# The tail of an attention and two-layer block: where z is widened and the tokens are split

## The chip, the cores and the metric

One core of one Trainium2 chip runs the whole kernel. The metric is the device time of one execution in microseconds (us), the median of several runs. The engines are TensorE (PE in the rows, its weight loads PEld), VectorE (DVE), ScalarE (ACT), GpSimd (POOL) and SyncE (SP), which issues most DMAs.

## The reference

The input passes through three stages; the change touches the last one only.

```
scores = q @ k^T / sqrt(D), masked to a window (half of the heads: a dilated one)
x   = softmax(scores) @ v                 # 2304 tokens x 512
h   = x @ w_in;  y = (h - tanh(h)) @ w_out          # 512 -> 2048 -> 512
h2  = y @ w_in2                                     # 512 -> 1024
sm  = softmax(h2);  s = h2 * sm
ln  = (s - mean(s)) / sqrt(var(s) + 1e-6) * g_ln
out = ln @ w_out2                                   # 1024 -> 512
```

## The kernel before

The order of instructions on each engine is the order of the program text; nothing reorders it. An engine that waits holds up all that stands behind it in its queue. Waits between engines are put in by the framework from what is read and written; a buffer of a pool is handed on when its last reader is done.

Attention and the middle layer are untouched; they end at about 507 us. The last stage works on nine pairs of token tiles of 128 (NP = 9, pairs 0 to 8). A pair has two tiles: 2i+1, called o in the text, and 2i, called e.

The **first product** of pair i, `mm3(i)` at L639, is h2 by a scheme of seven products instead of eight, with sums of blocks of y and of w_in2. Each product (`prod`, L615) is six matmuls of 512 columns, since each operand is split in a high and a low part and three of the four combinations are used. Four PSUM banks are used in turn: b0, b1, b2, b3. ScalarE copies b0 to c (L652); VectorE forms u2 (L653) and u3 (L658); four `neg_add` (L636) write the negated halves of both tiles to hn and keep a running minimum. The bank b1 is used again (product p4) once u2 has read it, b3 (p2) once u3 has read it. The list `mid` holds two hooks: hook 0 runs after b2's product and before u3, hook 1 after the first tile's minima. Behind them are the exponential (`softmax_e`, L681), the product with it (`softmax_u`, L686), the mean's removal (`softmax_z`, L692 and L693) and the sum of squares (`square`, L702).

The **second product**, `mm4` at L754, is 24 matmuls for each tile from z, the transposed and split normalised tile; its result is scaled by the factor g on ScalarE (L764) and written out by SP (L765).

z comes in one of two ways. `trz` (L723) transposes hn by TensorE into PSUM and splits it from there (L733, L734); pair 0 uses this. `split_z` (L736) makes a high and a low half of 16 bits (ScalarE L740, VectorE L741), SP starts a transposing DMA (L744), and `put_z` (L746) widens both halves (ScalarE L751, VectorE L752). In that way the tile is scaled by the factor f (column 4 of `sml`), in the first it is not, and `rest` multiplies g by it.

The **tokens' split**, `split_y(j, parts)` at L519, prepares y of pair j. Part 0 makes four differences on GpSimd (L530), one of them into y's own buffer, then casts one half (VectorE L537) and subtracts (GpSimd L538). Part 2 casts the other half, in which the fourth difference lies, and part 1 the sums; each has its L537 and L538. `load_y(j)` (L514) loads y of pair j by SP into the only buffer `yr`, which must have been read by the split of pair j-1. `fac` (L704) and `rest` (L710) make the factors f and g by small GpSimd instructions of [128x1].

The loop at L779 goes over the pairs: the factors and `split_z` of pair i+1, the second product of pair i, the first product of pair i+2. There the split of pair i+3 starts in hook 0 and is ended in the next turn of the loop, ahead of `split_z`.

Of the kernel before, what the change touches and what calls it, by code (L numbers as in the profile page):

```python
# [40 lines left out]
def tile_kernel(ctx: ExitStack, tc: tile.TileContext, qk, vw, cst, w_in, w_out, w_in2, w_out2, g_ln, out):  # L41
# [470 lines left out]
    NP = NTOK // YT  # L512

    def load_y(j):  # L514
        if j < NP:
            y_raw[j] = p2.tile([128, KD, YT], F32, tag="yr", name=f"yr{j}", bufs=1)
            nc.sync.dma_start(out=y_raw[j], in_=y_dr[:, :, j * YT:(j + 1) * YT])

    def split_y(j, parts=range(3)):  # L519

        if j >= NP:
            return
        r = y_raw[j]
        if 0 in parts:
            y = yt[j] = p2.tile([128, 2, 7, 2, TT], F32R, tag="yt", name=f"yt{j}")
            sm = y_sm[j] = p2.tile([128, 3, 2, TT], F32, tag="ysm", name=f"ysm{j}", bufs=1)
            a11, a21, a22 = r[:, 0:2, 0:TT], r[:, 0:2, TT:YT], r[:, 2:4, TT:YT]
            for o, a, b, op in ((sm[:, 0], a21, a22, ALU.add), (sm[:, 1], sm[:, 0], a11, ALU.subtract),
                                (sm[:, 2], a11, a21, ALU.subtract), (a21, r[:, 2:4, 0:TT], sm[:, 1], ALU.subtract)):
                nc.gpsimd.tensor_tensor(out=o, in0=a, in1=b, op=op)  # L530
        y, sm = yt[j], y_sm[j]
        yh = y[:, 0].rearrange("p s k t -> p (s k) t")
        yl = y[:, 1].rearrange("p s k t -> p (s k) t")
        for p, sl, v in ((0, slice(0, 4), r[:, :, 0:TT]), (2, slice(4, 8), r[:, :, TT:YT]),
                         (1, slice(8, 14), sm.rearrange("p s k t -> p (s k) t"))):
            if p in parts:
                nc.vector.tensor_copy(out=yh[:, sl], in_=v)  # L537
                nc.gpsimd.tensor_tensor(out=yl[:, sl], in0=v, in1=yh[:, sl].bitcast(F32), op=ALU.subtract)  # L538
        if 2 in parts:
            y_raw.pop(j)  # L540
            y_sm.pop(j)
# [73 lines left out]
    def prod(ps, y, blk, w, first=True):  # L615

        q = 0
        for kk in range(2):
            for a, b in ((0, 0), (0, 1), (1, 0)):
                nc.tensor.matmul(ps, y[:, a, blk, kk], w2i[w, kk][:, b], start=first and q == 0, stop=q == 5,  # L620
                                 skip_group_check=not first)
                q += 1

    def bank(pool, tag, i, nm):
        return pool.tile([128, 512], F32, tag=tag, name=f"s{nm}_{i}")

    def neg_add(i, t, n, a, b):

        d = st[2 * i + t]
        if "hn" not in d:  # L630
            d["hn"] = p3.tile([128, FF2], F32, tag="hn", name=f"hn{2 * i + t}", bufs=3)
            d["sml"] = p3.tile([128, 8], F32, tag="sml", name=f"sml{2 * i + t}", bufs=6)
            init, acc = 3.0e38, d["sml"][:, 7:8]
        else:
            init, acc = d["sml"][:, 7:8], d["sml"][:, 0:1]
        nc.vector.tensor_tensor_reduce(out=d["hn"][:, n * 512:(n + 1) * 512], in0=a, in1=b, op0=ALU.add, op1=ALU.min,  # L636
                                       scale=-1.0, scalar=init, accum_out=acc)

    def mm3(i, mid=()):  # L639

        y = yt.pop(i)
        for t in range(2):
            st[2 * i + t] = {}
        mid = dict(mid)
        b0, b1 = bank(sa, "b0", i, "p1"), bank(sa, "b1", i, "p6")
        prod(b0, y, 0, "b11")
        prod(b1, y, 5, "t2")
        u2 = p3.tile([128, 512], F32, tag="u2", name=f"u2_{i}", bufs=1)
        u3 = p3.tile([128, 512], F32, tag="u3", name=f"u3_{i}", bufs=1)
        b2, b3 = bank(sb, "b2", i, "p5"), bank(sb, "b3", i, "p7")  # L650
        c = p3.tile([128, 512], F32, tag="c", name=f"c_{i}", bufs=1)
        nc.scalar.copy(out=c, in_=b0)  # L652
        nc.vector.tensor_tensor(out=u2, in0=b1, in1=c, op=ALU.add)  # L653
        prod(b2, y, 4, "t1")
        if 0 in mid:
            mid[0]()
        prod(b3, y, 6, "t3")
        nc.vector.tensor_tensor(out=u3, in0=b3, in1=u2, op=ALU.add)  # L658
        neg_add(i, 1, 1, b2, u3)
        b1 = bank(sa, "b1", i, "p4")  # L660
        prod(b1, y, 3, "t4")
        neg_add(i, 1, 0, b1, u3)
        if 1 in mid:
            mid[1]()
        softmax_e(2 * i + 1)
        b3 = bank(sb, "b3", i, "p2")
        prod(b3, y, 1, "b21")
        neg_add(i, 0, 0, b3, c)
        softmax_u(2 * i + 1)
        prod(b2, y, 2, "b22", first=False)  # L670
        neg_add(i, 0, 1, b2, u2)
        softmax_e(2 * i)
        softmax_z(2 * i + 1)
        square(2 * i + 1)
        softmax_u(2 * i)
        softmax_z(2 * i)
# [33 lines left out]
    def rest(i):  # L710

        d = st[i]
        ssum, sc, var, g = (d["sml"][:, c:c + 1] for c in (1, 4, 5, 6))
        nc.gpsimd.tensor_scalar(out=ssum, in0=ssum, scalar1=1e-9, scalar2=1e-3, op0=ALU.add, op1=ALU.mult)
        nc.gpsimd.tensor_tensor(out=ssum, in0=ssum, in1=ssum, op=ALU.mult)
        nc.gpsimd.tensor_tensor(out=ssum, in0=ssum, in1=var, op=ALU.add)
        nc.gpsimd.tensor_tensor(out=ssum, in0=ssum, in1=half, op=ALU.pow)
        nc.gpsimd.tensor_tensor(out=var, in0=var, in1=sc, op=ALU.mult)
        nc.gpsimd.tensor_tensor(out=g, in0=ssum, in1=var, op=ALU.mult)
        if i < 2:  # L720
            nc.gpsimd.tensor_tensor(out=g, in0=g, in1=sc, op=ALU.mult)

    def trz(i):  # L723

        d = st[i]
        z = d["z"] = p3.tile([128, 2, NF2, TT], F32R, tag="z", name=f"z{i}")
        for n in range(2):
            ps = zo.tile([128, 512], F32, tag="zp", name=f"zp{i}_{n}").rearrange("p (j t) -> p j t", t=TT)
            for j in range(4):
                c = 4 * n + j  # L730
                nc.tensor.transpose(ps[:, j], d["hn"][:, c * TT:(c + 1) * TT], ident)
            zh, zl = z[:, 0, 4 * n:4 * n + 4], z[:, 1, 4 * n:4 * n + 4]
            nc.scalar.copy(out=zh, in_=ps)  # L733
            nc.vector.tensor_tensor(out=zl, in0=ps, in1=zh.bitcast(F32), op=ALU.subtract)  # L734

    def split_z(i):  # L736

        d = st[i]
        ab = p3.tile([128, 2, FF2], F16, tag="ab", name=f"ab{i}")
        nc.scalar.activation(out=ab[:, 0], in_=d["hn"], func=AF.Copy, scale=d["f"])  # L740
        nc.vector.scalar_tensor_tensor(out=ab[:, 1], in0=d["hn"], scalar=d["f"], in1=ab[:, 0], op0=ALU.mult,  # L741
                                       op1=ALU.subtract)
        t = d["zt"] = p3.tile([128, 2 * NF2, TT], F16, tag="zt", name=f"zt{i}")
        nc.sync.dma_start_transpose(out=t, in_=ab.rearrange("p a n -> p (a n)"))  # L744

    def put_z(i):  # L746

        d = st[i]
        z = d["z"] = p3.tile([128, 2, NF2, TT], F32R, tag="z", name=f"z{i}")
        t = d["zt"].rearrange("p (a j) t -> p a j t", a=2)  # L750
        nc.scalar.copy(out=z[:, 0], in_=t[:, 0])  # L751
        nc.vector.tensor_copy(out=z[:, 1], in_=t[:, 1])  # L752

    def mm4(i):  # L754
        d = st.pop(i)
        z = d["z"]
        po = zo.tile([128, DM], F32, tag="po", name=f"po{i}")
        q = 0
        for j in range(NF2):
            for a, b in ((0, 0), (0, 1), (1, 0)):  # L760
                nc.tensor.matmul(po, z[:, a, j], w2o[j][:, b], start=(q == 0), stop=(q == 3 * NF2 - 1))  # L761
                q += 1
        o = p3.tile([128, DM], F32, tag="o", name=f"o{i}")
        nc.scalar.activation(out=o, in_=po, func=AF.Copy, scale=d["g"])  # L764
        nc.sync.dma_start(out=out[i * TT:(i + 1) * TT, :], in_=o)  # L765

    mm3(0)
    fac(1)

# [9 lines left out]
    for i in range(NP):  # L779
        o, e = 2 * i + 3, 2 * i + 2  # L780
        if i + 1 < NP:
            square(e)
            fac(o)
            fac(e)
        split_y(i + 2, (1, 2))
        load_y(i + 3)
        if i + 1 < NP:
            split_z(o)
            split_z(e)
            rest(o)  # L790
            rest(e)
        mm4(2 * i + 1)
        if i + 1 < NP:
            put_z(o)
        mm4(2 * i)
        if i + 2 < NP:
            mm3(i + 2, {0: lambda: split_y(i + 3, (0,)), 1: lambda: put_z(e)})
        elif i + 1 < NP:
            put_z(e)
    p2.release()  # L800
    sa.release()

# [74 lines left out]
```

## Time and profile before

| | us |
|---|---|
| median of 3 runs | 721.9 (721.08 to 724.3) |
| the profiled execution | 726.59 |
| its span | 724.8 |
| TensorE busy | 690.9 (95%) |
| VectorE busy | 484.2 (67%) |
| ScalarE busy | 384.3 (53%) |
| GpSimd busy | 204.8 (28%) |

Times in the rows are us from the start of the span. A row in order of time begins with its start and its duration; where the engine stood idle just before, the idle time and what ended it stand at its end in brackets. The granted clock of TensorE is a share of its full speed of 2.4 GHz; the other level is 1.2 GHz.

### The profile page before, as it was taken

The page shows a single profiled execution, that of the slowest core. Times are in us where ns is not written, and L with a number is a line of the kernel's source. Part 1 is how long each engine was busy: PE and PEld are TensorE (multiplying, and loading weights), DVE is VectorE, ACT ScalarE, POOL GpSimd, SP SyncE. Part 2 cuts the span into 40 slices and gives each one's busy share as a digit, 9 for nine tenths or more (in the row PEclk, how much of TensorE's full clock was granted, in tenths as well). Part 3 has the DMA queues.
Part 4 walks back from the last instruction along what each step waited for, and adds up shares of the span by engine and source line. Part 5 has one row for each costly group of instructions (what it writes and reads, how often), then busy time and mean ns, then how long its engine had stood idle before and what let it go on. Part 6 is the DMA issues. An engine that isn't in the chain of part 4 may idle for free.

```text
span 724.8 us, 11261 instructions
## 1 busy us (share of the span) xinstructions
PE 690.9 (95%) x3978; PEld 636.4 (88%) x3978; DVE 484.2 (67%) x1157; ACT 384.3 (53%) x917; POOL 204.8 (28%) x274
## 2 busy tenths in 40 slices
PE   6898999999999999999999999999998989989987
PEld 5688999999999999999999999999876768777766
DVE  5987667476667766666667424998676757766760
ACT  5778776465555555555546433655444344534551
POOL 2312321111011111110011102661194774557530
PEclk9999999999999999999999999999999999999997
DMA  9985521232222122322112004532113551254322
GB/s 267 338 267 180 189 85 55 65 110 66 67 66 90 53 66 66 110 66 66 45 65 67 1 10 165 189 130 104 44 35 82 116 117 45 73 116 117 76 60 67
DMA packets 63591, 72.41 MB, mean 100 GB/s; under 512 B 36272, under 2 KB 50096, under 8 KB 63536
## 3 DMA queue, kind: packets, MB, share of 16 engines
q1 hardware_dynamic: 60368, 66.98, 31.9%
q10 hardware_dynamic: 3168, 4.72, 1.8%
q8 instruction: 31, 0.51, 0.3%
q14 instruction: 24, 0.20, 0.1%
HBM read 53.86 MB, written 9.44 MB: 87 GB/s over the span
## 4 chain that ended last, share of the span: by engine, by line
PE 73%; DVE 8%; DMA 6%; ACT 5%; issue 4%; POOL 2%; SPq 0%; ACTq 0%; POOLq 0%; DVEq 0%
PE y L381 28%; PE h L354 28%; PE sp L620 5%; DMA zt<-ab 5%; PE po L761 3%; PE pv L281 2%; PE qkp L205 2%; PE tp L260 2%; PE qkp L225 2%; ACT e L681 1%; DVE hn L636 1%; DMA qkr<-in_qk_dram 1%; DVE hn L686 1%; ACT e L702 1%; ACT ab L740 1%
## 5 line engine op out<-in xcount | busy, mean ns | idle before, releaser
L354 PE MATMUL h<-x,wi 128*128 128x384 f32 x1152 | 222.2, 341 | 1.3 <-DVE t L365 1.3
L381 PE MATMUL y<-gs,wo 128*128 128x384 f32 x1152 | 219.1, 339 | 0.0
L381 PEld LDWEIGHTS y<-gs,wo 128*128 128x128 f32 x1152 | 201.5, 189 | 1.8
L354 PEld LDWEIGHTS h<-x,wi 128*128 128x128 f32 x1152 | 200.2, 189 | 2.7 <-DVE t L365 1.5
L253 POOL TENSOR_TENSOR p<-p,rs 96x512 f32<-96x512 f32 x47 | 57.3, 1219 | 353.9 <-DVE rs L251 332.0
L761 PE MATMUL po<-w2o_o,z 128*128 128x512 f32 x432 | 103.2, 399 | 3.2 <-ACT z L751 3.2
L365 DVE TENSOR_TENSOR t<-h,t 128x384 f32<-128x384 f32 x96 | 53.0, 552 | 78.6 <-ACT t L362 78.5
L761 PEld LDWEIGHTS po<-w2o_o,z 128*128 128x128 f32 x432 | 83.1, 193 | 22.0 <-ACT z L751 3.6
L371 DVE TENSOR_TENSOR gs<-t,gs 128x384 fp32r<-128x384 f32 x96 | 82.6, 861 | 23.3 <-ACT gs L368 23.2
L362 ACT ACTIVATE t<-h 128x384 f32<-128x384 f32 x96 | 47.0, 489 | 93.9 <-PE h L354 90.6
L245 ACT ACTIVATE p<-p,nm 96x128 f32<-96x128 f32 x192 | 75.0, 393 | 21.5 <-DVE nm L210 21.1
L368 ACT CAST gs<-t 128x384 fp32r<-128x384 f32 x96 | 49.0, 510 | 49.4 <-DVE t L365 49.1
L620 PE MATMUL sp<-w2i_t,yt 128*128 128x512 f32 x216 | 56.0, 410 | 13.2 <-DVE u L653 12.5
L620 PEld LDWEIGHTS sp<-w2i_t,yt 128*128 128x128 f32 x216 | 41.4, 195 | 25.0 <-DVE u L653 15.4
L741 DVE SCALAR_TENSOR_TENSOR ab<-hn,sml,ab 128x1024 f16<-128x1024 f32 x16 | 37.4, 2375 | 14.2 <-ACT ab L740 14.2
L681 ACT ACTIVATE e<-hn,sml 128x1024 f32<-128x1024 f32 x18 | 20.8, 1154 | 44.9 <-DVE sml L636 26.2
L751 ACT CAST z<-zt 128x1024 fp32r<-128x1024 f16 x16 | 16.8, 1048 | 49.8 <-DMA zt<-ab 49.6
L620 PE MATMUL sp<-w2i_b,yt 128*128 128x512 f32 x162 | 41.5, 403 | 0.0
L620 PEld LDWEIGHTS sp<-w2i_b,yt 128*128 128x128 f32 x162 | 32.1, 199 | 7.2
L205 PE MATMUL qkp<-qkr 64*96 64x128 f32 x160 | 29.4, 339 | 7.8 <-DMA qkr<-in_qk_dram 6.6
L245 ACT ACTIVATION_READ_ACCUMULATOR p<-p,nm 96x1 f32 x192 | 36.2, 189 | 0.0
L205 PEld LDWEIGHTS qkp<-qkr 64*96 64x96 f32 x160 | 24.1, 205 | 12.4 <-DMA qkr<-in_qk_dram 6.0
(89 smaller groups left out, 844.9 us busy)
## 6 DMA issues: line engine op xcount, KB each, us to landing
qkr<-in_qk_dram SPq DMA_DIRECT2D x28, 448.0 KB, 3.3
raw_wi<-in_w_in_dram SPq DMA_DIRECT2D x16, 511.8 KB, 7.5
raw_wo<-in_w_out_dram SPq DMA_DIRECT2D x16, 511.8 KB, 7.5
v<-in_vw_dram SPq DMA_DIRECT2D x48, 128.0 KB, 3.3
y_dr<-ys ACTq DMA_DIRECT2D x6, 768.0 KB, 3.9
yr<-y_dr SPq DMA_DIRECT2D x9, 512.0 KB, 4.7
out_dram<-o SPq DMA_DIRECT2D x18, 256.0 KB, 2.2
qkr<-in_qk_dram SPq DMA_DIRECT2D x20, 224.0 KB, 5.4
```

The source lines that it names most:

```text
L205: nc.tensor.matmul(ps[:, b], d["r"][:64, b * NQ:(b + 1) * NQ], d["r"][:64, QC + b * NK:QC + (b + 1) * NK], start=True, stop=True)
L245: nc.scalar.activation(out=d["p"][:, b], in_=d["p"][:, b], func=AF.Exp, scale=-1.0, bias=d["nm"][:, b:b + 1], accum_out=d["sm"][:, b:b + 1])
L253: eng.tensor_tensor(out=d["p"], in0=d["p"], in1=d["rs"].unsqueeze(2).to_broadcast([NQ, 4, NK]), op=ALU.mult)
L354: nc.tensor.matmul(ps, w[:, a, k * 128:(k + 1) * 128], xt[g, k][:, b], start=(n == 0), stop=(n == 3 * KD - 1))
L362: nc.scalar.activation(out=t, in_=ps, func=AF.Tanh)
L365: nc.vector.tensor_tensor(out=t, in0=ps, in1=t, op=ALU.subtract)
L368: nc.scalar.copy(out=gs[:, 0], in_=t)
L371: nc.vector.tensor_tensor(out=gs[:, 1], in0=t, in1=gs[:, 0].bitcast(F32), op=ALU.subtract)
L381: nc.tensor.matmul(yb[g][m], wo[c][:, a, m * 128:(m + 1) * 128], gs[:, b], start=(c == 0 and i == 0), stop=(c == NF - 1 and i == 2))
L620: nc.tensor.matmul(ps, y[:, a, blk, kk], w2i[w, kk][:, b], start=first and q == 0, stop=q == 5, skip_group_check=not first)
L741: nc.vector.scalar_tensor_tensor(out=ab[:, 1], in0=d["hn"], scalar=d["f"], in1=ab[:, 0], op0=ALU.mult, op1=ALU.subtract)
L761: nc.tensor.matmul(po, z[:, a, j], w2o[j][:, b], start=(q == 0), stop=(q == 3 * NF2 - 1))
```

## The change

Three things are changed. From the fourth pair on (first product i = 3, which splits pair 4) all of the split of the next pair stands inside the first product, part 0 ahead of c and u2 and parts 2 and 1 behind u2, with the load of the pair after that behind it; the splits of pairs 2 and 3 stay where they were, but the loads of pairs 3 and 4 now stand behind `split_z` and `rest`. The widening of o's z moves from between the two second products into hook 0 of the next first product. For the last pair, z of both tiles is transposed by TensorE (`trz`) behind the second products of pair 7, and `rest` multiplies its g by the factor.

```diff
@@ mm3 @@
         prod(b0, y, 0, "b11")
         prod(b1, y, 5, "t2")
+        if i > 2:
+            split_y(i + 1, (0,))
...
         nc.scalar.copy(out=c, in_=b0)
         nc.vector.tensor_tensor(out=u2, in0=b1, in1=c, op=ALU.add)
+        if i > 2:
+            split_y(i + 1, (1, 2))
+            load_y(i + 2)
         prod(b2, y, 4, "t1")
@@ rest @@
-        if i < 2:
+        if i // 2 in (0, NP - 1):
             nc.gpsimd.tensor_tensor(out=g, in0=g, in1=sc, op=ALU.mult)
@@ loop over the pairs @@
-        split_y(i + 2, (1, 2))
-        load_y(i + 3)
-        if i + 1 < NP:
+        if i < 2:
+            split_y(i + 2, (1, 2))
+        if i + 2 < NP:
             split_z(o)
             split_z(e)
+        if i + 1 < NP:
             rest(o)
             rest(e)
+        if i < 2:
+            load_y(i + 3)
         mm4(2 * i + 1)
-        if i + 1 < NP:
-            put_z(o)
+        if i + 2 == NP:
+            trz(o)
         mm4(2 * i)
+        if i + 2 == NP:
+            trz(e)
         if i + 2 < NP:
-            mm3(i + 2, {0: lambda: split_y(i + 3, (0,)), 1: lambda: put_z(e)})
-        elif i + 1 < NP:
-            put_z(e)
+            mm3(i + 2, {0: lambda: (put_z(o), i == 0 and split_y(3, (0,))), 1: lambda: put_z(e)})
```

## Rows read from the trace of the kernel before

**Rows 1.** Costliest groups of the page: busy, mean ns, idle before and its releaser.
```profile
L620 PE MATMUL sp<-w2i_t,yt 128*128 128x512 f32 x216 | 56.0, 410 | 13.2 <-DVE u L653 12.5
...
L751 ACT CAST z<-zt 128x1024 fp32r<-128x1024 f16 x16 | 16.8, 1048 | 49.8 <-DMA zt<-ab 49.6
```
**Rows 2.** In order of time, VectorE, pairs 2, 3, 7 and 8.
```profile
549.53 0.68 DVE L658 TENSOR_TENSOR u<-sp,u 128x512 f32<-128x512 f32 x1
...
555.38 0.75 DVE L636 CUSTOM_DVE_ANT_0 hn<-sp,u,sml 128x512 f32<-128x512 f32 x1
...
572.12 0.69 DVE L653 TENSOR_TENSOR u<-sp,c 128x512 f32<-128x512 f32 x1 [1.38 <-ACT c L652]
...
573.44 0.68 DVE L658 TENSOR_TENSOR u<-sp,u 128x512 f32<-128x512 f32 x1
...
578.28 0.75 DVE L636 CUSTOM_DVE_ANT_0 hn<-sp,u,sml 128x512 f32<-128x512 f32 x1
...
672.29 0.75 DVE L636 CUSTOM_DVE_ANT_0 hn<-sp,u,sml 128x512 f32<-128x512 f32 x1
...
693.34 0.75 DVE L636 CUSTOM_DVE_ANT_0 hn<-sp,u,sml 128x512 f32<-128x512 f32 x1
```
**Rows 3.** In order of time, TensorE's weight loads and last matmuls.
```profile
597.32 2.21 PEld L620 LDWEIGHTS sp<-w2i_t,yt 128*128 128x128 f32 x6 [4.03 <-DVE u L653]
...
602.63 10.94 PEld L761 LDWEIGHTS po<-w2o_o,z 128*128 128x128 f32 x48
...
644.74 4.24 PEld L620 LDWEIGHTS sp<-w2i_b,yt 128*128 128x128 f32 x12
...
706.88 14.02 PE L761 MATMUL po<-w2o_o,z 128*128 128x512 f32 x48 [3.16 <-ACT z L751]
```
**Rows 4.** Stretches: PE, PEld, DVE, ACT, POOL busy, clock, DMA share, GB/s.
```profile
576.90:602.63 25.73, 22.12 (x91) 17.81 (x90) 16.36 (x28) 10.63 (x17) 14.27 (x23) 0.93 0.40 82
...
692.35:724.80 32.45, 25.39 (x98) 19.99 (x96) 8.57 (x14) 10.19 (x14) 6.65 (x16) 0.87 0.26 65
```
**Rows 5.** The transpositions of pair 0: ns min/median/max, first and last start.
```profile
L731 PE MATMUL zp<-cst_sb,hn x16: 271/273/273, 521.5 to 525.9; 128*128 128x128 f32 x16
```
**Rows 6.** In order of time, the second run of eight transpositions.
```profile
525.15 1.04 PE L731 MATMUL zp<-cst_sb,hn 128*128 128x128 f32 x8
```
**Rows 7.** In order of time, SP: the transposing DMAs' issue in the first two pairs.
```profile
540.79 5.14 SPq L744 DMA_TRANSPOSE zt<-ab  x2
...
564.27 5.63 SPq L744 DMA_TRANSPOSE zt<-ab  x2
```
**Rows 8.** The loads of L517, from issue to landing.
```profile
DMA to landing us min/median/max: 4.3/4.6/4.9
```
**Rows 9.** In order of time, GpSimd: a split's first and last steps, the last factor.
```profile
571.01 0.73 POOL L530 TENSOR_TENSOR ysm<-yr 128x256 f32<-128x256 f32 x1
...
574.08 1.29 POOL L538 TENSOR_TENSOR yt<-yr,yt 128x512 fp32r<-128x512 f32 x1
...
705.28 0.19 POOL L719 TENSOR_TENSOR sml<-sml 128x1 f32<-128x1 f32 x1
```
**Rows 10.** In order of time, VectorE and GpSimd where they overlap.
```profile
622.46 1.29 POOL L538 TENSOR_TENSOR yt<-yr,yt 128x512 fp32r<-128x512 f32 x1
...
623.23 1.07 DVE L752 CAST z<-zt 128x1024 fp32r<-128x1024 f16 x1
...
680.04 2.84 POOL L538 TENSOR_TENSOR yt<-ysm,yt 128x768 fp32r<-128x768 f32 x1
...
681.09 2.87 DVE L741 SCALAR_TENSOR_TENSOR ab<-hn,sml,ab 128x1024 f16<-128x1024 f32 x1
```
**Rows 11.** VectorE's casts from 500 us on: ns min/median/max, first and last start.
```profile
L537 DVE CAST yt<-yr x14: 417/422/803, 524.3 to 676.5; 128x512 fp32r<-128x512 f32 x14
L537 DVE CAST yt<-ysm x7: 552/553/555, 535.3 to 676.9; 128x768 fp32r<-128x768 f32 x7
...
L752 DVE CAST z<-zt x16: 687/694/1073, 546.2 to 708.1; 128x1024 fp32r<-128x1024 f16 x16
```

## The prediction

> **What bounds the kernel now.** I read the busy shares by stage first, then the costliest groups, then the tail in order of time; the change touches nothing before about 540 us. The page shows who waits: ScalarE's widening of z idles 49.8 us for the transposing DMA, and the matmuls of the first product idle 13.2 us, 12.5 of it for u2 [rows 1]. In order of time the reason is plain: the copy c of the next first product stands behind the widening of z in ScalarE's queue, so u2 comes only after the DMA (572.12 for u2, 573.44 for u3 [rows 2]), while TensorE waits up to 4.03 us and then loads six weights in 2.21 us [rows 3]. That stretch of 25.73 us has a mean granted clock of 0.93, so part of it ran at 1.2 instead of 2.4 GHz [rows 4]. With no wait, a pair is 90 matmuls at 10.94/48 us = 20.5 us [rows 3].
>
> I count in one mark, N: the start of the last minimum of a pair (neg_add on the other tile's second half). Before, N is 555.38 for pair 2, 578.28 for pair 3, 672.29 for pair 7 and 693.34 for pair 8 [rows 2]. So pairs 4 to 7 took 94.0 us, 23.5 each, 3.0 over TensorE's 20.5. That is the most that the change can win there, 12 us in all, and only if nothing else takes the place of the DMA wait.
>
> **The end: a gain.** The last two second products wait 3.16 us for z and then take 14.02 us for 48 matmuls, which at full clock are 10.94 [rows 3]. From the start of pair 7's second product (692.35 [rows 4]) to the last matmul (720.90) is 28.6 us. After, TensorE makes both transpositions itself: 96 matmuls, 21.9 us, and 16 transpositions. The nearest row has 16 of them as single instructions of 0.27 us that issue in two runs of eight, a run 1.04 us; I take 2.1 us, at most 16 x 0.27 = 4.4 [rows 5, 6]. 24.1 us in all: 4.5 us are won (2.2 at the upper bound). The four evictions of each transposition on ScalarE and VectorE lie beside a second product of 5.5 us; the added multiplication by sc is one [128x1] on GpSimd, long before it is needed. Both at nothing.
>
> **Pairs 2 and 3: a loss in the changeover.** load_y(3) and load_y(4) move from ahead of the two transposing DMAs in SP's queue to behind them. SP is held by these two for 5.14 us from 540.79 and 5.63 us from 564.27 [rows 7]. So load_y(3) is issued at 545.9, some 6 us later than before, and lands 4.6 us later [rows 8], at 550.6. The split's cast stands ahead of u3 in VectorE's queue, so u3, which was at 549.53 [rows 2], starts at about 551.2, and pair 2's N goes from 555.4 to about 556.4.
>
> Pair 3 is worse, since its whole split now stands inside its own first product (the changed code takes "i > 2" in the fourth one): the cast of part 0 is ahead of u2, the two others ahead of u3. SP is done with the transposing DMAs at 569.9 [rows 7]; plus the 1.0 us of pair 2, less some 0.5 as no load competes with them, load_y(4) is issued at 570.5 and lands at 575.2. u2, which was at 572.12, comes at 576. What is late next is u3. GpSimd's four differences start when the load has landed and take 3.1 us (571.01 to 574.08 [rows 9]), 0.3 more for the cast beside them: 578.6. Only then may VectorE cast parts 2 and 1.
>
> **What the casts cost there.** VectorE and GpSimd don't run side by side on SBUF here. A widening that takes 0.69 us alone took 1.07 where GpSimd's L538 was on: it began at 623.23 and ended at 624.30, 0.55 after L538 ended at 623.75 [rows 10]. The split of z that began at 681.09 ended at 683.96, 1.08 after the L538 that ended at 682.88 [rows 10]. The cast is 0.42 alone and up to 0.80 [rows 11]. I read this as a whole instruction of one holding the other up. The Trainium skill says so too (SBUF — State Buffer, "SBUF: two separate sides"): the shared pair of ports is an exclusive lock, taken for the instruction by whichever engine starts first. By that rule the sum below holds; if the two only shared, rival A's sum would.
>
> With it, from the end of the differences: GpSimd's L538 of part 0 follows at once (1.3), the cast of part 2 waits it out and needs 0.3 more, the cast of part 1 about 0.5, then L538 of part 2, waiting since the first cast, goes ahead (1.2), and only then VectorE's widening of z (0.55 left of 0.69 [rows 11]): 3.8 us until u3, against 0.42 + 0.55 + 0.69 = 1.6 with no hold-up. u3 of pair 3 is at 582.4. From u3 to N the old pair 3 took 4.84 us (573.44 to 578.28 [rows 2]); I take 5.1, since TensorE has idled 4 us ahead of its last 12 matmuls, and such 12, 2.7 us at full clock, took 4.24 behind one wait [rows 3]. N of pair 3 is 587.5, 9.2 us later than before.
>
> **Pairs 4 to 7: a new chain of the same length.** The DMA is off the path: by pair 8's rows z is usable 13.5 us after N (693.34 to 706.88 [rows 2, 3]), early enough. But GpSimd's queue now holds, in this order, both fac, both rest, the four differences, three L538. The factors end 12.1 us after N (pair 8's last one at 705.28 + 0.19, and there too no L538 stood between [rows 9]); the differences need 3.1; then 3.8 as above to u3; then 4.84 to 5.1 to the next N: 12.1 + 3.1 + 3.8 + 5.0 = 24.0 us, against 23.5. Four pairs: +2.0 us. Bounds: 21.8 without the hold-up, 24.8 if the last 12 matmuls run at the lower clock and the small GpSimd steps lose a us more. I take 24.0, as both rows of an overlap show the whole hold-up. load_y(j+2) behind that split on SP is free: the next transposing DMAs come some 8 us later, and it lands long before the next split.
>
> Pair 8 has no split beside it, so there TensorE decides: 20.5 us from pair 7's second product, which starts about 0.7 us ahead of N. From N of pair 7 to pair 8's end this is 19.8 against 20.1 (672.29 to 692.35 [rows 2, 4]): -0.3.
>
> **The sum.** +9.2 (changeover) + 2.0 (pairs 4 to 7) - 0.3 (pair 8) - 4.5 (end) = +6.4 us. The profiled execution took 726.59 with its span of 724.8, 4.7 over the median of the runs; I add the difference to the median: 721.9 + 6.4 = 728.3.
>
> **Rivals.**
> A. The casts are not held up. u3 of pair 3 comes at 580.0 and N at 585.0 (+6.7), pairs 4 to 7 take 21.8 each (-6.8): 6.7 - 6.8 - 0.3 - 4.5 = -4.9, 717.0 us, faster. For it: u2 and the minima, which read PSUM, run beside GpSimd undelayed. Against: the overlaps above [rows 10, 11]. Chance 0.17.
> B. Held up once, not twice: the widening of z gets in ahead of L538 of part 2. 22.9 a pair, pair 3 at +8.0: 8.0 - 2.4 - 0.3 - 4.5 = +0.8, 722.7, no change. It decides by who goes when a cast ends. Against: L538 of part 1 at 680.04 took 2.84, far more than 1.5 times the 1.29 of one of two thirds its size [rows 10], so there VectorE got in between two of GpSimd's, the one that waits first. Chance 0.18.
> C. load_y(4) lands in time for the fourth split. Then the differences start when the factors end, at about 572.1 instead of 575.2, and 3.1 us fall away: +3.3, 725.2. Against: SP's order. Chance 0.08.
> D. 24.8 a pair: +9.6, 731.5. For it: TensorE now idles 3.6 us in every pair, and its clock fell in both stretches with waits as long. Chance 0.12.
> The forecast has 0.45.
>
> **How the numbers follow.** A measurement tells 0.5% (3.6 us: 718.3 to 725.5) from no change. Slower: the forecast's and D's, less what their own spread brings below 725.5, with part of C: 0.58. Same: B, most of C and the edge of the forecast: 0.24. Faster: A and a little of B: 0.18. The forecast's own range is 725 to 731; 717 to 732 leaves out about half of A and some of D.
>
> **What would show it.** Right: u2 of the fourth pair at about 576, its u3 past 582; the wait for z from the DMA gone from ScalarE, and in its place VectorE's casts waiting for GpSimd's differences and lasting up to 1.3 us longer than alone; TensorE idle before p2 (b3), not before p4; about 24 us from N to N; TensorE without a gap in the last 24 us and at full clock. Wrong: N to N at 21.8 or less, or load_y(4) issued ahead of the transposing DMAs.

## The result: slower by 1.5%, and why the range just missed it

Before 721.49 us (median of 4), after 732.68 (median of 4, 730.74 to 734.97): the ratio is 1.015, 95% interval 1.0107 to 1.0194. Timed once more side by side on another occasion, the two took 721.94 and 733.86, ratio 1.0147 (1.0117 to 1.0177). Slower was forecast, by 6.4 us; it is 11 to 12, and the median lies 0.7 above the range.

The profiled executions stand nearer to the forecast: the span went from 724.8 to 731.8, 7.0 more, at the same mean granted clock of 0.985. So the chain that was worked out is there nearly step by step, and most of the miss is in what before's profiled execution was taken for. Both are shown below.

**The profile after.** In order of time on VectorE, the fourth first product (u2, now L655, to u3, now L663), then N of pairs 2 to 7, which answer to [rows 2]:

```profile
575.76 0.43 DVE L537 CAST yt<-yr 128x512 fp32r<-128x512 f32 x1 [7.30 <-DMA yr<-y_dr]
576.10 0.68 DVE L655 TENSOR_TENSOR u<-sp,c 128x512 f32<-128x512 f32 x1
579.11 1.48 DVE L537 CAST yt<-yr 128x512 fp32r<-128x512 f32 x1 [2.32 <-POOL yr L530]
580.50 0.55 DVE L537 CAST yt<-ysm 128x768 fp32r<-128x768 f32 x1
580.97 1.75 DVE L757 CAST z<-zt 128x1024 fp32r<-128x1024 f16 x1
582.64 0.68 DVE L663 TENSOR_TENSOR u<-sp,u 128x512 f32<-128x512 f32 x1
...
556.81 0.74 DVE L636 CUSTOM_DVE_ANT_0 hn<-sp,u,sml 128x512 f32<-128x512 f32 x1
...
588.10 0.75 DVE L636 CUSTOM_DVE_ANT_0 hn<-sp,u,sml 128x512 f32<-128x512 f32 x1
...
611.77 0.75 DVE L636 CUSTOM_DVE_ANT_0 hn<-sp,u,sml 128x512 f32<-128x512 f32 x1
...
636.04 0.75 DVE L636 CUSTOM_DVE_ANT_0 hn<-sp,u,sml 128x512 f32<-128x512 f32 x1
...
659.70 0.75 DVE L636 CUSTOM_DVE_ANT_0 hn<-sp,u,sml 128x512 f32<-128x512 f32 x1
...
683.96 0.75 DVE L636 CUSTOM_DVE_ANT_0 hn<-sp,u,sml 128x512 f32<-128x512 f32 x1
```

VectorE waits 7.30 us for y of pair 4 (the row shows the wait ahead of the cast) and 2.32 us for GpSimd's differences; u2 is at 576.10 (forecast: 576), u3 at 582.64 (582.4), N of pair 3 at 588.10 (587.5). From there N to N is 23.67, 24.27, 23.66 and 24.26 us (24.0).

SP shows where the load stands, to be read beside [rows 7]:

```profile
565.70 4.75 SPq L749 DMA_TRANSPOSE zt<-ab  x2
570.56 0.99 SPq L517 DMA_DIRECT2D yr<-y_dr  x1
```

The load is issued when the second transposing DMA has left SP, at 570.56 (forecast: 570.5).

All engines in order of time, pair 5's split inside the fifth first product:

```profile
602.58 0.74 POOL L530 TENSOR_TENSOR yr<-yr,ysm 128x256 f32<-128x256 f32 x1
...
603.28 1.30 POOL L538 TENSOR_TENSOR yt<-yr,yt 128x512 fp32r<-128x512 f32 x1
603.36 1.50 DVE L537 CAST yt<-yr 128x512 fp32r<-128x512 f32 x1 [0.86 <-POOL yr L530]
604.78 0.55 DVE L537 CAST yt<-ysm 128x768 fp32r<-128x768 f32 x1
604.94 1.52 POOL L538 TENSOR_TENSOR yt<-yr,yt 128x512 fp32r<-128x512 f32 x1 [0.36 <-DVE yt L537]
605.25 1.76 DVE L757 CAST z<-zt 128x1024 fp32r<-128x1024 f16 x1
606.42 2.27 POOL L538 TENSOR_TENSOR yt<-ysm,yt 128x768 fp32r<-128x768 f32 x1
...
606.93 0.68 DVE L663 TENSOR_TENSOR u<-sp,u 128x512 f32<-128x512 f32 x1
```

This is the double hold-up of the forecast. The cast of part 2 starts 0.08 us behind GpSimd's L538 and ends 0.28 us after it; it takes 1.50, and alone 0.42 [rows 11]. L538 of part 2, whose row starts at 604.94, goes ahead of the widening of z, which takes 1.76 instead of 0.69. From the end of the differences (603.32) to u3 it is 3.61 us; 3.8 was the forecast.

TensorE's weight loads and last matmuls, beside [rows 3]:

```profile
576.84 2.21 PEld L620 LDWEIGHTS sp<-w2i_t,yt 128*128 128x128 f32 x6 [4.45 <-DVE u L655]
...
583.37 4.17 PEld L620 LDWEIGHTS sp<-w2i_b,yt 128*128 128x128 f32 x12 [4.33 <-DVE u L663]
...
607.67 2.59 PEld L620 LDWEIGHTS sp<-w2i_b,yt 128*128 128x128 f32 x12 [2.31 <-DVE u L663]
...
631.31 4.10 PEld L620 LDWEIGHTS sp<-w2i_b,yt 128*128 128x128 f32 x12 [3.27 <-DVE u L663]
...
709.57 1.03 PE L736 MATMUL zp<-cst_sb,hn 128*128 128x128 f32 x8
...
716.74 11.25 PE L766 MATMUL po<-w2o_o,z 128*128 128x512 f32 x48
```

The wait for u2 ahead of p4 has become a wait for u3 ahead of p2 in the pairs that carry a split; pair 3 has both (4.45 and 4.33 us). ScalarE still idles for z's DMA, 14.4 us in all instead of 49.6, but no u2 waits for its copy c any more. At the end TensorE transposes in runs of 1.03 us and has its last 48 matmuls at full clock, 11.25 instead of 14.02.

### The profile page after: what moved, and what is told of

The parts are those of the page before. It is cut to its first block, busy times and chain, and to the rows that moved or that the text cites. A ratio compares the mean times of both kernels' runs of the same rounds, so it can differ in the third digit from the quotient of the medians.

```text
span 731.8 us, 11282 instructions
## 1 busy us (share of the span) xinstructions
PE 692.7 (95%) x3994; PEld 638.2 (87%) x3994; DVE 479.0 (65%) x1157; ACT 383.9 (52%) x917; POOL 205.8 (28%) x276
## 4 chain that ended last, share of the span: by engine, by line
PE 73%; DVE 9%; POOL 8%; issue 4%; ACT 3%; DMA 2%; SPq 0%; ACTq 0%; POOLq 0%; DVEq 0%
PE y L381 28%; PE h L354 26%; PE po L766 6%; PE sp L620 5%; PE pv L281 2%; PE tp L260 2%; PE qkp L225 2%; PE qkp L205 2%; POOL ysm L530 1%; DMA yr<-y_dr 1%; POOL yt L538 1%; DVE z L757 1%; DVE hn L636 1%; DVE p L210 1%; ACT e L686 1%
## 5 line engine op out<-in xcount | busy, mean ns | idle before, releaser
L766 PE MATMUL po<-w2o_o,z 128*128 128x512 f32 x432 | 100.7, 392 | 0.0
L766 PEld LDWEIGHTS po<-w2o_o,z 128*128 128x128 f32 x432 | 81.1, 188 | 17.7
L245 ACT ACTIVATE p<-p,nm 96x128 f32<-96x128 f32 x192 | 75.2, 394 | 21.2 <-DVE nm L210 20.8
L620 PE MATMUL sp<-w2i_b,yt 128*128 128x512 f32 x162 | 46.6, 440 | 17.3 <-DVE u L663 17.3
L620 PEld LDWEIGHTS sp<-w2i_b,yt 128*128 128x128 f32 x162 | 34.3, 216 | 27.7 <-DVE u L663 20.1
L620 PE MATMUL sp<-w2i_t,yt 128*128 128x512 f32 x216 | 52.6, 398 | 4.8 <-DVE u L655 4.0
L292 DVE TENSOR_TENSOR x<-pv,x 128x384 fp32r<-128x384 f32 x24 | 16.4, 703 | 25.7 <-ACT x L290 25.2
L746 DVE SCALAR_TENSOR_TENSOR ab<-hn,sml,ab 128x1024 f16<-128x1024 f32 x14 | 22.2, 1630 | 15.9 <-ACT ab L745 15.9
```

The source lines that it names most:

```text
L245: nc.scalar.activation(out=d["p"][:, b], in_=d["p"][:, b], func=AF.Exp, scale=-1.0, bias=d["nm"][:, b:b + 1], accum_out=d["sm"][:, b:b + 1])
```

## Experiments

One table for all profiled executions, worked out from N (its start, on VectorE) and from the end of the last matmul, in us. The first number is the time of N of pair 1; the next three columns are from N to N; the last one is the median of before's own runs that were timed beside that kernel. Rows with the same one were timed together.

| kernel | N of pair 1 | pair 2 | pair 3 | pairs 4-7 | N of pair 7 to last matmul | median | before's |
|---|---|---|---|---|---|---|---|
| before | 530.74 | 24.64 | 22.90 | 94.01 | 48.61 | 721.49 | |
| before again | 530.78 | 24.49 | 22.32 | 92.98 | 47.57 | 724.28 | 723.94 |
| before, third | 531.50 | 26.07 | 22.76 | 91.42 | 47.35 | (one) 724.79 | 721.94 |
| after | 530.51 | 26.30 | 31.29 | 95.86 | 44.03 | 732.68 | 721.49 |
| after again | 532.88 | 26.33 | 32.27 | 94.52 | 43.21 | 733.86 | 721.94 |
| loads back | 529.00 | 22.48 | 27.47 | 95.67 | 44.25 | 724.40 | 723.94 |
| low order | 528.95 | 26.39 | 30.25 | 91.98 | 44.26 | 728.38 | 721.94 |
| end only | 530.73 | 24.87 | 22.50 | 93.20 | 44.22 | 720.15 | 721.94 |
| widening only | 529.53 | 22.40 | 20.11 | 84.86 | 45.88 | 709.06 | 723.94 |
| widening and end | 528.78 | 22.48 | 20.98 | 86.07 | 42.95 | 706.29 | 723.94 |

**Before, again.** No edit.

> The kernel before, unchanged, profiled once more. Open: the profiled execution of before took 726.59 us, 5 over the median of its runs, while that of the changed kernel took 733.56, about its median. Theory 1: TensorE's clock fell in more pairs of the last stage in that execution than in a usual one (stretches of 25.98, 25.73 and 24.43 us with a mean granted clock of 0.93 beside 21.9 to 22.4 at 1.00); then a faster execution shows fewer such stretches, its mean clock over the span is above 0.985, and the runs' times go down as their clocks go up. Theory 2: the excess lies ahead of 530 us; then the stretches of the last stage are as before and the last stage starts some us earlier.

Ratio 1.000 (0.998 to 1.002). Its profiled execution, with a clock of 0.991, took 723.83 us. Pair 6's first product, that of [rows 3] at 644.74, shows the difference (weight loads, then the last matmuls):

```profile
642.58 1.23 PEld L620 LDWEIGHTS sp<-w2i_t,yt 128*128 128x128 f32 x6 [2.40 <-DVE u L653]
643.88 2.67 PEld L620 LDWEIGHTS sp<-w2i_b,yt 128*128 128x128 f32 x12
...
705.13 13.01 PE L761 MATMUL po<-w2o_o,z 128*128 128x512 f32 x48 [3.13 <-ACT z L751]
```

The twelve loads that took 4.24 us in the first profile take 2.67 here, and the last 48 matmuls 13.01 instead of 14.02. Up to N of pair 1 the two agree within 0.04 us. Of the executions of before that were timed beside it, the three with a clock of 0.985 took 726.17 to 726.92, the three with 0.995 took 720.95 to 722.50. So the 726.59 of the first profile (0.985) is one of the slowest that this kernel has on record, by the clock in its last stage: theory 1.

**The widening only.** Before, with the widening of o's z in hook 0 and nothing else:

```diff
         mm4(2 * i + 1)
-        if i + 1 < NP:
+        if i + 2 == NP:
             put_z(o)
         mm4(2 * i)
         if i + 2 < NP:
-            mm3(i + 2, {0: lambda: split_y(i + 3, (0,)), 1: lambda: put_z(e)})
+            mm3(i + 2, {0: lambda: (put_z(o), split_y(i + 3, (0,))), 1: lambda: put_z(e)})
```

> Before, with one part of the change alone: the widening of o's z moves into hook 0 of the next first product, ahead of the split's part 0; the split, the loads and the end stay as they were. Theory (the split's move and not that of the widening is what lost the time): c and u2 no longer wait for the transposing DMA, the factors and the split stay where VectorE and GpSimd had time for them, a pair takes 20.6 to 22 us from N to N instead of 23.5, TensorE hardly waits: faster by 9 to 16 us, 706 to 713. Rival (the widening in hook 0 is itself late, since u3 stands behind it): a pair stays at 23 to 24 us and the time within 3 us of before.

709.06 us, ratio 0.9826 (0.9775 to 0.9877): the theory holds. Pairs 4 to 7 take 84.9 us, 21.2 each. So this part of the change, alone, is worth some 13 to 15 us; what loses it again is the move of the split and of its loads, which the next runs take apart.

**The widening and the end.** The edit above, with the change's own edit of the end (`trz` for pair 8).

> Before, with the move of the widening and with TensorE's transposition of the last pair, without the split's and the loads' move. Theory: the gains add, 4.5 us on top of the one before: 701 to 709. Rival (the widening in hook 0 is late): 4.5 us faster than before at most, 717.

706.29 us, ratio 0.9775 (0.9744 to 0.9807), the fastest of all, 17.7 us under before and some 26 under the changed kernel. The end adds 2.8 us to the gain of the widening alone, where 4.5 were expected. Stretches from one second product to the next (the columns of [rows 4]):

```profile
548.84:569.81 20.97, 20.96 (x92) 16.75 (x90) 16.61 (x26) 10.64 (x16) 14.34 (x24) 1.00 0.42 101
569.81:594.22 24.41, 22.23 (x92) 17.59 (x91) 18.35 (x28) 11.07 (x17) 15.93 (x25) 0.95 0.41 87
594.22:615.11 20.89, 20.89 (x92) 17.18 (x91) 15.10 (x23) 10.76 (x15) 14.24 (x23) 0.98 0.43 102
615.11:635.88 20.77, 20.77 (x91) 16.82 (x90) 16.22 (x27) 10.46 (x15) 13.28 (x22) 1.00 0.44 101
...
656.61:677.12 20.51, 20.51 (x92) 16.90 (x91) 16.15 (x27) 11.28 (x17) 12.99 (x20) 1.00 0.34 78
```

TensorE is busy in nearly all of each, which take 20.5 to 21.0 us; one pair is left out of step, where z's DMA was late (its first product waits 2.60 us for u3, and the stretch has a clock of 0.95).

**Loads back.** The changed kernel with load_y(3) and load_y(4) where they were:

```diff
         if i < 2:
             split_y(i + 2, (1, 2))
+            load_y(i + 3)
...
-        if i < 2:
-            load_y(i + 3)
         mm4(2 * i + 1)
```

> The changed kernel with load_y(3) and load_y(4) back ahead of the transposing DMAs, all else as changed. Theory (the loads' place made pairs 2 and 3 late): N of pair 2 comes 4 us earlier than in the changed kernel, N of pair 3 some 8 us earlier (580 instead of 588), then 24 us a pair as before: 8 us faster than the changed kernel, 724 to 726. Rival (the split inside the first product costs that pair as much wherever the load stands): pair 3's N stays within 3 us of 588, and the time at 729 or more.

724.40 us, ratio to before 1.0027 (1.0004 to 1.0050). That is 8.3 us less than the changed kernel's 732.68, which was not timed beside it; by the two ratios to before it is 8.9. Pairs 2 and 3 together take 49.95 instead of 57.59 us, 7.6 less; pairs 4 to 7 are as slow as in the changed kernel. Pair 3 still takes 27.5, since the split itself stands in it. VectorE, and TensorE's loads behind it, show for what:

```profile
569.68 1.47 DVE L537 CAST yt<-yr 128x512 fp32r<-128x512 f32 x1 [4.77 <-POOL yr L530]
...
573.21 0.68 DVE L663 TENSOR_TENSOR u<-sp,u 128x512 f32<-128x512 f32 x1
```

```profile
573.94 4.54 PEld L620 LDWEIGHTS sp<-w2i_b,yt 128*128 128x128 f32 x12 [6.97 <-DVE u L663]
```

With y there in time, the cast still waits 4.77 us for the differences, which stand behind the factors in GpSimd's queue.

This kernel and the one with the widening and the end, timed together, differ in nothing but the split's place from pair 4 on: 724.40 against 706.29. So the split's move costs 18.1 us by itself, and the loads' move 8 to 9 on top of it.

**Low order.** The changed kernel with GpSimd's L538 in the order 2, 1, 0:

```diff
-    def split_y(j, parts=range(3)):
+    def split_y(j, parts=range(3), low0=True):
...
             if p in parts:
                 nc.vector.tensor_copy(out=yh[:, sl], in_=v)
-                nc.gpsimd.tensor_tensor(out=yl[:, sl], in0=v, in1=yh[:, sl].bitcast(F32), op=ALU.subtract)
+                if p or low0:
+                    nc.gpsimd.tensor_tensor(out=yl[:, sl], in0=v, in1=yh[:, sl].bitcast(F32), op=ALU.subtract)
+        if 2 in parts and not low0:
+            nc.gpsimd.tensor_tensor(out=yl[:, 0:4], in0=r[:, :, 0:TT], in1=yh[:, 0:4].bitcast(F32), op=ALU.subtract)
...
-            split_y(i + 1, (0,))
+            split_y(i + 1, (0,), False)
...
-            split_y(i + 1, (1, 2))
+            split_y(i + 1, (1, 2), False)
```

> The changed kernel with GpSimd's three L538 in the order 2, 1, 0 instead of 0, 2, 1, so that no L538 stands between the four differences and the cast of part 2. Theory (one engine holds up the other for a whole instruction, twice in each pair): the cast of part 2 takes 0.42 instead of 1.50, u3 comes 1.1 us earlier, N to N is 22.9 instead of 24.0 in pairs 4 to 7, and with pair 3 the kernel is 5 us faster than the changed one. Rival (the casts are late for the differences alone): N to N stays at 24.

728.38 us, 5.5 less than the changed kernel beside it (733.86). Pairs 4 to 7 take 22.99, 22.96, 22.95 and 23.08 us, as the theory has it. VectorE, pair 5's split:

```profile
600.82 0.43 DVE L537 CAST yt<-yr 128x512 fp32r<-128x512 f32 x1 [0.81 <-POOL yr L530]
601.16 0.56 DVE L537 CAST yt<-ysm 128x768 fp32r<-128x768 f32 x1
601.63 1.78 DVE L760 CAST z<-zt 128x1024 fp32r<-128x1024 f16 x1
603.33 0.68 DVE L666 TENSOR_TENSOR u<-sp,u 128x512 f32<-128x512 f32 x1
```

The first cast is 0.43 us instead of 1.50, the second hold-up stays (1.78): the same work in another order on another engine moves the whole kernel by 5 us. That shows the first hold-up; the second one is read from the rows alone, as no run takes it away by itself.

GpSimd's end of the differences (600.79) and the widening of the second tile, behind u3:

```profile
600.05 0.74 POOL L530 TENSOR_TENSOR yr<-yr,ysm 128x256 f32<-128x256 f32 x1
...
605.57 1.34 DVE L760 CAST z<-zt 128x1024 fp32r<-128x1024 f16 x1
```

From the end of the differences to u3 it is 2.54 us instead of 3.61, the 1.1 that was expected. But the low part that now comes last holds up the second widening (1.34 instead of 0.69), so that u3 to N takes 0.4 more: a pair gains about 0.6 us on the 23.6 of the changed kernel timed beside it.

**The end only.** Before with `trz` for pair 8, its `split_z` and `put_z` left out, and the factor in `rest`:

```diff
-        if i + 1 < NP:
+        if i + 2 < NP:
             split_z(o)
             split_z(e)
...
         mm4(2 * i + 1)
-        if i + 1 < NP:
+        if i + 2 < NP:
             put_z(o)
+        elif i + 2 == NP:
+            trz(o)
         mm4(2 * i)
+        if i + 2 == NP:
+            trz(e)
...
```

> Before with one part of the change alone: z of the last pair transposed by TensorE. Theory: 4.5 us by the profiled execution of before (28.6 us from pair 7's second product to the last matmul against 24.1), 3 to 4.5 us in the median, since the clock fell in that stretch by differing amounts (12.58 and 13.59 us for the last 48 loads). Rival (the gain is given back by the transpositions and their evictions): within 1 us of before.

720.15 us, ratio 0.9968 (0.9953 to 0.9984), 2.3 us by the ratio: less than the 3 to 4.5 expected of the median, but a gain. From N of pair 7 to the last matmul it takes 44.22 us, against 47.35 to 48.61 in the three profiles of before: 3.1 to 4.4.

**After, again, and before, a third time.** No edits; they were timed together with the two last experiments.

> The changed kernel, unchanged, timed beside before on another chip. Theory (the miss is in what before's profiled execution was taken for, not in the chain): N to N is 23.6 to 24.3 again in pairs 4 to 7, and the kernel is 8 to 11 us slower than before, less than the 11.2 of the first runs if before's median is nearer to 724. Rival (the steps of the sum are wrong by themselves): N to N is elsewhere than 24, or the difference is 11 or more again with before at 724.

> The kernel before, profiled a third time, to see which stretches vary. Theory: the stages ahead of 507 us agree within 2 us, and the pairs whose wait for u2 is over 2.4 us vary by 1 to 3 us with the lower clock behind it; rival: the stretches of the last stage agree and the rest varies.

The chain is there again (23.62 to 23.66 from N to N), but the difference is 11.9 us with before at 721.94: the expectation of 8 to 11 is missed. In the third profile of before pairs 4 to 7 take 91.4 us, 2.6 less than in the first, pair 2 takes 1.4 more, and N of pair 1 is 0.76 later: the last stage varies most, but in more than the pairs with the longest waits.

## Why the prediction was right, and where it was wrong

Against the profile on which it was worked out, by its own terms (forecast, then after less before from the table):

| term | forecast | measured |
|---|---|---|
| changeover, pairs 2 and 3 | +9.2 | +10.05 |
| pairs 4 to 7 | +2.0 | +1.85 |
| pair 8 and the end | -4.8 | -4.58 |
| sum | +6.4 | +7.3 |

With the -0.2 ahead of pair 2 and -0.1 behind the last matmul, that is the 7.0 us by which the span grew.

**Right.** The load behind the transposing DMAs (8 to 9 us by its own run); the differences, the casts and the widening as the new chain in place of the DMA wait (24.0 us a pair, 23.97 measured); the hold-up of a whole instruction, twice (its first half 5.5 us by its own run); the end. The casts' 1.50 and 1.76 us agree with what the Trainium skill says (SBUF — State Buffer, "SBUF: two separate sides"): the shared ports are an exclusive lock for a whole instruction. Of the rivals, A and B are refuted by N to N and by the rows, which show both hold-ups. C's price, 3.1 us for the load in time, was too low: the run gives 7.6 for the two pairs, 3.8 each, since C left pair 2 out and that load is as late. D's 731.5 lies nearest to the median, but not by its way: no pair takes its 24.8.

**Partly luck.** That 23.97 falls on the forecast's 24.0. From the factors to u3 the chain is 0.2 shorter than forecast, and a pair takes 23.67 us where TensorE's last twelve loads ran at full clock (2.59 us), 24.27 where they did not (4.10); it was two pairs of each. In the second profile of the changed kernel all four ran at full clock and took 23.62 to 23.66, 0.4 under the forecast.

**Mis-sized, in the sum.** The changeover, by 0.85 us. Pair 2 took 1.7 instead of 1.0 more. Behind its u3 the product L691, 1.23 us alone, was held up by L538 for 0.9 us, which was not counted:

```profile
551.77 4.60 PE L620 MATMUL sp<-w2i_b,yt 128*128 128x512 f32 x12 [4.21 <-DVE u L663]
...
554.51 1.28 POOL L538 TENSOR_TENSOR yt<-yr,yt 128x512 fp32r<-128x512 f32 x1
...
554.73 2.15 DVE L691 SCALAR_TENSOR_TENSOR hn<-hn,e 128x1024 f32<-128x1024 f32 x1
```

It explains at most about 0.4 of the miss there: the last twelve matmuls, behind a wait of 4.21 us for u3, took 4.60 and ended only at 556.37, 0.44 ahead of N. Pair 3 took 0.2 more: its last twelve loads ran in 4.17 us behind a wait of 4.33, and from u3 to N it was 5.46, not 5.1. One estimate was wrong without harm: the next transposing DMAs come 13 to 14 us behind the load of the new split, not 8.

**Wrong: the carrying over to the median.** This is the step that failed. "I add the difference to the median" takes it that the difference is the same in every execution of before. It is not. Before's profiled execution, 726.59 us, stands 5.1 over its median of 721.49, and the changed kernel's, 733.56, only 0.9 over its own: these 4.2 us, and the 0.6 by which the span grew more than forecast, are the whole way from 6.4 to 11.2. Before's profiled execution had a clock of 0.985 and was among the slowest; its timed ones lie between 720.4 and 726.9, at 0.985 to 0.995. The changed kernel waits over 4 us in pairs 2 and 3 in both of its profiles, and its eight executions have 0.981 to 0.988, 730.7 to 735.0. At like clocks the two differ by about what the profiles show: at 0.988, 730.74 against 724.51 to 725.06; at 0.985, 733.56 and 734.77 against 726.17 to 726.92. This sorts executions by their clock after the fact; no run sets the clock. By it, most of the rest of the 11 us is that before mostly runs at a better clock than in the execution from which 94.0 us and 28.6 us were read. With the other two profiles of before (and the mean of both of after), pairs 2 and 3 lose 10.3 us instead of 9.2, pairs 4 to 7 lose 3.0 instead of 2.0, and the end with pair 8 wins 3.8 instead of 4.8: +9.4. The range had no term for this; its upper end came from the chain alone.

**What stays open.** About 2 us of the difference of the medians are not in these terms. N of pair 1, ahead of anything that was changed, lies between 528.8 and 532.9 in the ten profiles, in no order of the kernels; so this may be such variation, but no run settles it. Nor does any show what decides whether the clock falls behind a wait.

## What to carry to other kernels

A wait that goes away uncovers the next one: before moving work into a gap, write down each queue's order behind the move, and follow every load, cast and small step to the instruction that now stands behind it. The part of this change that only let the copy pass the DMA wait was worth 13 to 15 us by itself; the move of the split cost 18, and that of its loads 8 to 9 more. And before a difference is carried from a profile to a median, ask where that execution's clock stands among the timed ones.

## What the runs showed of the hardware that was not expected

The length of a wait does not decide by itself whether the clock falls. In before, the wait of 2.42 us in pair 6 was followed by six loads at the full rate and then twelve in 4.24 us; in its second profile 2.40 us in the same place by six and twelve (2.67) at the full rate; in its third, 3.41 us in pair 4 by six loads in 1.23, the full rate. In the changed kernel, 3.27 us ahead of twelve loads left them 4.10 us, and in its second profile 3.20 us in the same place left them 2.59. The rows of before, of its third profile and of the changed kernel's second one:

```profile
643.40 1.23 PEld L620 LDWEIGHTS sp<-w2i_t,yt 128*128 128x128 f32 x6 [2.42 <-DVE u L653]
...
598.74 1.23 PEld L620 LDWEIGHTS sp<-w2i_t,yt 128*128 128x128 f32 x6 [3.41 <-DVE u L653]
...
634.65 2.59 PEld L620 LDWEIGHTS sp<-w2i_b,yt 128*128 128x128 f32 x12 [3.20 <-DVE u L663]
```
